# Four edits and a new set of offsets in a planned attention-plus-two-FFN kernel on one core

## The chip, the cores and the metric

The kernel runs on one core of one Trainium2 chip. The metric is device microseconds of one execution; the figure quoted is the median of three runs. The profile comes from one further execution, of which both the device time and the span (first to last instruction) are given.

## The reference, cut to what matters

A delta-rule attention (4 batches, 8 heads, 768 tokens, head width 48) gives 3072 rows of 384, and two feed-forward layers (384 to 2048 to 384) follow.

```python
for t in range(S):                       # 768 steps, state (B, H, 48, 48)
    y[:, :, t] = q_t @ state
    state = state + bt * outer(kt, vt - state.T @ kt)    # kt of norm 1
x = y as (3072, 384)
h = x @ w1_in;  x = np.maximum(0.01 * h, h) @ w1_out
h = x @ w2_in;  out = (h - np.tanh(h)) @ w2_out
```

## The kernel before, in words

The sequence is cut into 12 chunks n of 64 tokens, and two neighbouring chunks form a pair u = n // 2. For each pair the kernel normalises the keys (`keys`, for pair 0 `first_keys`), turns them so that the head width lies on the partitions (`t_batch`), and multiplies them with themselves (`g_batch`, the grams). It inverts a unit triangular matrix for each of the heads (`inverses`: 32x32 blocks, column by column on VectorE), and `merges` joins two blocks into the matrix T: a first round of 32x32 matmuls into PM, a second one whose result is copied into the corner of T. Each chunk then goes through `queries`, `products`, `states` (the recurrence from chunk to chunk) and `outputs`, which leaves x, 256 tokens (two per partition) by 384.

The FFN works on these 256 tokens at a time, once per layer, so there are 24 layer runs. All its matmuls are fp16 with every operand as a pair hi + lo and three products (hi hi, hi lo, lo hi). `to_xa` prepares x of the first layer: a sum of squares on ScalarE, a matmul with ones that spreads the total over the partitions (`norm_sum`), a power-of-two scale (`pow2_scale`), the hi part on ScalarE and the lo part on VectorE, and then a turn by DMA (for chunk 0 by TensorE). `to_xb` does so between the layers. A layer run has 8 steps: `h_part` (18 matmuls of 256 columns, L609 in the profile, into ps_h) and, three steps later, `o_part` (12 of 384 columns into ps_o).

The weights arrive as 64-bit words and are converted at the start by `weight`: three VectorE operations a part (`w_f32`), a sum of squares, a scale and the split into hi and lo. Matrices 0 and 1 (first layer) come first, 2 and 3 after.

Nothing is issued in the order of the code. Every instruction is recorded as a node (L609 and L612 are the two lines that issue all of them), and a planner (`tails`, `schedule`) orders each engine's queue from its cost tables, from the room in the rings of buffers and from the table `BIAS`, an offset for each stage and chunk. So an engine's queue is a fixed list, in which work of several stages is interleaved. Ring `s_r` (six rooms, "sx" in the profile) serves the FFN's intermediate results, the hi and lo parts and the landing tiles of turned keys; ring `ps_a` has four PSUM banks for all small matmuls.

Two ranges matter for the keys. For chunks in `K_DMA` (2 to 11) `t_batch` makes an fp16 pair of the keys (four VectorE and ScalarE operations into KH), turns both halves by DMA into landing tiles of `s_r`, and adds them on VectorE into the fp32 tile kt. For the others (0 and 1) it multiplies with an identity in fp32 and copies two PSUM banks into kt. `M8` (pairs 2 to 5) are the pairs whose merges use eight tiles of the array at a time; pairs 0 and 1 use four.

```python
hi, lo = (KH[:, c_, :, :, 0:D] for c_ in range(2))        # L1010, chunks in K_DMA
    copy(hi[:, :, g], kn[:, :, g])                        # ScalarE
    tt(lo[:, :, g], kn[:, :, g], hi[:, :, g], ALU.subtract)
    turn(land[c_]..., KH[:, c_]...)                       # DMA transpose on SP's queue
tt(kt..., land[0], land[1], ALU.add)
```

Of the kernel before, what the change touches and what calls it, by code (L numbers as in the profile page):

```python
# [19 lines left out]
KS = 64.0  # L20
# [10 lines left out]
def layers(n):  # L31
# [11 lines left out]
OUTB = range(2, 12)  # L43
TRACE = ()
# [3 lines left out]
K_DMA = range(2, 12)  # L48
# [8 lines left out]
    ('consts', 0): -2.8, ('dma', 'b', 0): -10.37, ('dma', 'b', 1): 39.25, ('dma', 'grams', 10): 0.6,  # L57
    ('dma', 'grams', 11): -45.81, ('dma', 'grams', 2): 61.53, ('dma', 'grams', 3): -110.94,
    ('dma', 'grams', 4): 13.52, ('dma', 'grams', 5): -1.77, ('dma', 'grams', 6): 46.0,
    ('dma', 'grams', 7): -43.11, ('dma', 'grams', 8): -183.14, ('dma', 'grams', 9): -82.57,  # L60
    ('dma', 'k', 0): 8.15, ('dma', 'k', 1): 85.3, ('dma', 'keys', 10): -62.96, ('dma', 'keys', 11): 11.27,
    ('dma', 'keys', 2): 130.34, ('dma', 'keys', 3): -19.83, ('dma', 'keys', 4): -117.06,
    ('dma', 'keys', 5): -51.02, ('dma', 'keys', 6): -0.27, ('dma', 'keys', 7): -41.62,
    ('dma', 'keys', 8): -33.98, ('dma', 'keys', 9): -40.04, ('dma', 'o_part1', 0): -113.06,
# [7 lines left out]
    ('dma', 'queries', 0): -146.73, ('dma', 'queries', 1): 17.69, ('dma', 'queries', 10): -116.19,
    ('dma', 'queries', 11): 10.95, ('dma', 'queries', 2): -28.97, ('dma', 'queries', 3): -147.71,
    ('dma', 'queries', 4): -53.56, ('dma', 'queries', 5): 11.09, ('dma', 'queries', 6): -62.06,
    ('dma', 'queries', 7): 5.92, ('dma', 'queries', 8): -44.59, ('dma', 'queries', 9): 63.43,
    ('dma', 'to_xa', 1, 1): -72.81, ('dma', 'to_xa', 10, 1): -8.26, ('dma', 'to_xa', 11, 1): 154.84,
    ('dma', 'to_xa', 2, 1): 2.93, ('dma', 'to_xa', 3, 1): 5.4, ('dma', 'to_xa', 4, 1): 32.04,
    ('dma', 'to_xa', 5, 1): 3.58, ('dma', 'to_xa', 6, 1): 16.44, ('dma', 'to_xa', 7, 1): -144.99,
    ('dma', 'to_xa', 8, 1): -22.03, ('dma', 'to_xa', 9, 1): 22.28, ('dma', 'to_xb', 0, 1): -131.12,
    ('dma', 'to_xb', 1, 1): -169.83, ('dma', 'to_xb', 10, 1): -107.58, ('dma', 'to_xb', 11, 1): 50.71,  # L80
    ('dma', 'to_xb', 2, 1): -7.15, ('dma', 'to_xb', 3, 1): -6.01, ('dma', 'to_xb', 4, 1): -20.2,
    ('dma', 'to_xb', 5, 1): 65.65, ('dma', 'to_xb', 6, 1): -16.83, ('dma', 'to_xb', 7, 1): -97.29,
    ('dma', 'to_xb', 8, 1): 34.46, ('dma', 'to_xb', 9, 1): -4.63, ('dma', 'v', 0): -65.53,
    ('dma', 'weight', 0, 0): -46.39, ('dma', 'weight', 0, 1): -40.51, ('dma', 'weight', 0, 2): -23.2,
    ('dma', 'weight', 0, 3): 21.56, ('dma', 'weight', 0, 4): 56.7, ('dma', 'weight', 0, 5): -5.62,
    ('dma', 'weight', 1, 0): -159.92, ('dma', 'weight', 1, 1): -183.08, ('dma', 'weight', 1, 2): -28.75,
    ('dma', 'weight', 1, 3): -35.61, ('dma', 'weight', 1, 4): -172.45, ('dma', 'weight', 1, 5): -164.56,
    ('dma', 'weight', 2, 0): -32.76, ('dma', 'weight', 2, 1): -6.37, ('dma', 'weight', 2, 2): 4.29,
    ('dma', 'weight', 2, 3): -15.49, ('dma', 'weight', 2, 4): -23.36, ('dma', 'weight', 2, 5): -0.69,
    ('dma', 'weight', 3, 0): 5.74, ('dma', 'weight', 3, 1): -258.17, ('dma', 'weight', 3, 2): -95.47,  # L90
    ('dma', 'weight', 3, 3): -26.22, ('dma', 'weight', 3, 4): 24.43, ('dma', 'weight', 3, 5): -55.49,
    ('first_keys', 0): 59.37, ('grams', 0): 63.14, ('grams', 0, 1): 177.07, ('grams', 1): -205.35,
# [10 lines left out]
    ('h_part1', 9): -0.9, ('inverses', 0): 47.06, ('inverses', 0, 1): 30.6, ('inverses', 1): -11.12,  # L103
    ('inverses', 1, 1): -390.76, ('inverses', 2): -4.07, ('inverses', 2, 1): 225.04, ('inverses', 3): 19.08,
    ('inverses', 3, 1): -0.34, ('inverses', 4): 42.84, ('inverses', 4, 1): -93.8, ('inverses', 5): 2.69,
    ('inverses', 5, 1): -33.82, ('k', 0): -3.88, ('k', 1): -69.27, ('keys', 10): 147.22, ('keys', 11): 55.65,
    ('keys', 2): -18.98, ('keys', 3): -163.15, ('keys', 4): 65.04, ('keys', 5): -252.2, ('keys', 6): 84.49,
    ('keys', 7): -27.36, ('keys', 8): 67.06, ('keys', 9): -58.78, ('merges', 0): -11.68, ('merges', 1): 195.64,
    ('merges', 2): 144.45, ('merges', 3): 2.47, ('merges', 4): -7.63, ('merges', 5): -10.32,
# [16 lines left out]
    ('states', 6, 2): -20.49, ('states', 7): 1.72, ('states', 7, 1): -230.9, ('states', 7, 2): 48.97,
# [1385 lines left out]
```

## Time and profile before

| | |
|---|---|
| median of 3 runs (lowest, highest) | 966.23 us (964.88, 966.59) |
| profiled execution, device time | 965.78 us |
| its span | 963.6 us |
| busy share of TensorE, VectorE, ScalarE | 93%, 63%, 52% |
| mean granted TensorE clock | 0.969 of full speed |

Shares of the whole span hide that this kernel has two parts. In the first 110 us the weights and the first pairs are prepared; from then on the FFN's matmuls run. The rows below are read part by part.

### The profile page before, as it was taken

The page shows a single profiled execution, that of the slowest core. Times are in us where ns is not written, and L with a number is a line of the kernel's source. Part 1 is how long each engine was busy: PE and PEld are TensorE (multiplying, and loading weights), DVE is VectorE, ACT ScalarE, POOL GpSimd, SP SyncE. Part 2 cuts the span into 40 slices and gives each one's busy share as a digit, 9 for nine tenths or more (in the row PEclk, how much of TensorE's full clock was granted, in tenths as well). Part 3 has the DMA queues.
Part 4 walks back from the last instruction along what each step waited for, and adds up shares of the span by engine and source line. Part 5 has one row for each costly group of instructions (what it writes and reads, how often), then busy time and mean ns, then how long its engine had stood idle before and what let it go on. Part 6 is the DMA issues. An engine that isn't in the chain of part 4 may idle for free.

```text
span 963.6 us, 29002 instructions
## 1 busy us (share of the span) xinstructions
PE 896.5 (93%) x12756; PEld 677.5 (70%) x12756; DVE 608.6 (63%) x1332; ACT 499.5 (52%) x1187; POOL 4.9 (1%) x22
## 2 busy tenths in 40 slices
PE   2346899999999999999999999999999999999997
PEld 2215777778777777777777777777777768777675
DVE  7999999987984458953253598499322344512342
ACT  7657767666357566346362427544334434524342
POOL 1000000000000000000000000000000000000000
PEclk9586799999999999999999999999999999999999
DMA  9983673325022432121012111212021000300000
GB/s 349 402 235 104 193 181 116 108 67 95 23 74 59 71 90 64 21 56 36 18 41 33 55 41 36 50 31 56 17 56 18 3 19 17 52 1 18 17 18 16
DMA packets 86718, 71.30 MB, mean 74 GB/s; under 512 B 61760, under 2 KB 73024, under 8 KB 86592
## 3 DMA queue, kind: packets, MB, share of 16 engines
q1 hardware_dynamic: 86592, 69.46, 27.1%
q8 instruction: 99, 1.62, 0.7%
q14 instruction: 27, 0.22, 0.1%
HBM read 44.14 MB, written 4.72 MB: 51 GB/s over the span
## 4 chain that ended last, share of the span: by engine, by line
PE 79%; DVE 13%; ACT 4%; issue 2%; DMA 1%; SPq 1%; ACTq 0%; DVEq 0%
PE ps_h L609 36%; PE ps_o L609 35%; PE ps_a L609 8%; DVE xi L612 3%; DVE wo L612 3%; DVE wi L612 3%; DVE gd L612 2%; ACT gd L612 1%; DVE g L612 1%; DMA wo<-in_w_in_dram 1%; ACT sx L612 1%; DVE sx L612 1%; ACT XW L612 1%; ACT jk L612 1%; ACT wo L612 1%
## 5 line engine op out<-in xcount | busy, mean ns | idle before, releaser
L609 PE MATMUL ps_h<-x,wi 128*128 128x256 f16 x3456 | 403.6, 273 | 3.1 <-ACT sx L612 2.6
L609 PE MATMUL ps_o<-wo,g 128*128 128x384 f16 x2304 | 400.9, 326 | 0.2 <-issue 0.2
L609 PEld LDWEIGHTS <-wi 128*128 128x128 f16 x3456 | 334.9, 98 | 57.3 <-issue 4.5
L609 PEld LDWEIGHTS <-g 128*128 128x128 f16 x2304 | 221.9, 98 | 132.9 <-issue 0.5
L612 ACT ACTIVATE g<-sx 128x512 f16<-128x512 f32 x192 | 120.3, 628 | 113.0 <-PE ps_o L609 57.6
L612 DVE TENSOR_TENSOR g<-sx,g 128x512 f16<-128x512 f32 x96 | 66.0, 688 | 112.6 <-ACT g L612 112.0
L612 DVE SCALAR_TENSOR_TENSOR sx<-sx,kap,ps_h 128x512 f32<-128x512 f32 x96 | 71.2, 744 | 66.8 <-ACT sx L612 66.3
L612 ACT ACTIVATE sx<-ps_h 128x512 f32<-128x512 f32 x96 | 56.7, 592 | 91.8 <-PE ps_h L609 63.2
L612 ACT ACTIVATE sx<-ps_h,kap 128x512 f32<-128x512 f32 x96 | 65.1, 681 | 73.7 <-PE ps_h L609 63.4
L612 DVE SCALAR_TENSOR_TENSOR g<-sx,g 128x512 f16<-128x512 f32 x96 | 66.0, 688 | 36.4 <-ACT g L612 36.0
L612 DVE TENSOR_TENSOR gd<-xi 128x30 f32<-128x30 f32 (+9 forms) x180 | 59.2, 329 | 3.5
L612 DVE TENSOR_TENSOR xi<-xi,gd 128x30 f32<-128x30 f32 (+9 forms) x180 | 59.1, 329 | 3.5
L612 ACT ACTIVATE jk<-kf 128x48 bf16<-128x48 f32 x160 | 38.4, 240 | 14.3 <-DMA kf<-in_k_dram 10.7
L612 ACT ACTIVATE sx<-x,sxs 128x768 f16<-128x768 f32 (+1 forms) x26 | 22.7, 881 | 22.1 <-DVE sxs L612 22.1
L612 ACT ACTIVATION_READ_ACCUMULATOR jk<-kf 128x1 f32 x160 | 30.0, 187 | 0.0
L612 DVE SCALAR_TENSOR_TENSOR wi<-wo,wi 128x768 int32<-128x768 int32 x32 | 29.8, 950 | 0.0
L609 PE MATMUL ps_a<-q,kt 48*64 48x64 f32 x768 | 15.1, 229 | 13.8 <-DMA q<-in_q_dram 11.4
L612 DVE SCALAR_TENSOR_TENSOR sx<-x,sxs,sx 128x768 f16<-128x768 f32 (+1 forms) x26 | 24.6, 951 | 4.6 <-ACT sx L612 4.4
L612 ACT ACTIVATE sx<-x 128x768 bf16<-128x768 f32 x24 | 20.2, 840 | 13.7 <-DVE x L612 13.4
L612 ACT ACTIVATE gd<-ps_a 32x256 f32<-32x256 f32 (+1 forms) x72 | 23.9, 373 | 5.2 <-PE ps_a L609 4.6
L609 PEld LDWEIGHTS ps_a<-q,kt 48*64 48x64 f32 x768 | 13.3, 142 | 16.6 <-ACT wo L612 11.5
L612 DVE TENSOR_SCALAR sx<-ps_o,kap 128x384 f32<-128x384 f32 x12 | 7.4, 618 | 27.5 <-PE ps_o L609 25.5
(124 smaller groups left out, 730.2 us busy)
## 6 DMA issues: line engine op xcount, KB each, us to landing
wo<-in_w_in_dram SPq DMA_DIRECT2D x32, 384.0 KB, 7.8
q<-in_q_dram SPq DMA_DIRECT2D x12, 512.0 KB, 4.5
wi<-in_w_out_dram SPq DMA_DIRECT2D x14, 384.0 KB, 7.8
kf<-in_k_dram SPq DMA_DIRECT2D x12, 384.0 KB, 3.4
vf<-in_v_dram SPq DMA_DIRECT2D x12, 384.0 KB, 3.4
out_dram<-sx SPq DMA_DIRECT2D x48, 96.0 KB, 2.2
x<-in_w_out_dram SPq DMA_DIRECT2D x10, 384.0 KB, 4.0
b<-in_beta_dram SPq DMA_DIRECT2D x6, 512.0 KB, 4.7
```

Source lines behind the costliest of these rows:

```text
L609: self.eng["pe"].matmul(out=o.real(), lhsT=lhsT.real(), rhs=rhs.real(), start=start, stop=stop)
L612: getattr(self.eng[n.on], op)(**{k: v.real() if isinstance(v, View) else v for k, v in kw.items()})
```

## The change

`K_DMA` becomes range(4, 12): chunks 2 and 3 (the second pair) get their keys turned by TensorE, as chunks 0 and 1 did. `PAIRS` is new: for chunks 4 to 11 `g_batch` multiplies the two landing tiles of fp16 keys in three products instead of the fp32 tile kt with itself (kt is still made, for `products` and `states`). `merges` of pairs 0 and 1 does its two rounds and their copies for one half of the heads and then for the other, each under a stage of its own; pairs 2 to 5 are as before. `to_xa` takes a scale for each token instead of one for the 256: two sums of squares, one for each token of a partition, no `norm_sum`, and the hi and lo parts in two operations each for every chunk (before, for chunks 0 and 1 only). `to_xb` multiplies by the inverse of that scale as it copies the layer's result, and `kappa` has one operation less. The table `BIAS` is new in all its values, and some constants of the planner's cost tables change. `SPLIT` and `BY_PE`, with the code that they guard, are empty.

```diff
+SPLIT = ()
+BY_PE = ()
+PAIRS = range(4, 12)
-K_DMA = range(2, 12)
+K_DMA = range(4, 12)
 BIAS = {
-    ('consts', 0): -2.8, ('dma', 'b', 0): -10.37, ('dma', 'b', 1): 39.25, ('dma', 'grams', 10): 0.6,
+    ('consts', 0): -163.33, ('dma', 'b', 0): -14.31, ('dma', 'b', 1): 4.88, ('dma', 'grams', 10): 101.49,
...
     def pow2_scale(o, sq, top, inv=None, by=1):
-        t = g_.tile(p2_r, [128, 2], F32)
-        ts(t[:, 0:1], sq, 2.0 ** -80, None, ALU.max)
+        w = o.shape[1]
+        t = g_.tile(p2_r, [128, 4], F32)
+        ts(t[:, 0:w], sq, 2.0 ** -80, None, ALU.max)
...
             tt(kt.rearrange("p m h i -> p (m h i)"), land[0], land[1], ALU.add)
+            land_t[n] = [t.rearrange("p (m h i) -> p m h i", m=GM, h=2) for t in land]
             return
...
         for m in range(GM):
+            if n in PAIRS:
+                for a, b in ((0, 0), (0, 1), (1, 0)):
+                    for g, h in TILES:
+                        node = mm(ps2[g][HS[h], m], land[a][HD[g], m, h], land[b][HD[g], m, h], a + b == 0, a == 1)
+                continue
             for g, h in TILES:
-                mm(ps2[g][HS[h], m], kt[HD[g], m, h], kt[HD[g], m, h])
+                node = mm(ps2[g][HS[h], m], kt[HD[g], m, h], kt[HD[g], m, h])
...
+        else:
+            for f in range(2):
+                g_.stage = "merges", u, f
+                for jobs, out in ((first, middle), (second, corner)):
+                    ps = bank(HB)
+                    g_.cut()
+                    for m in range(GM):
+                        for h in range(2):
+                            jobs(ps, m, m + f * GM, HQ[2 * h], HQ[2 * h + 1], *spots(f, h))
+                    out(f, ps)
...
-        if n in BOTH or i:
+        if i:
             copy(w[0], x, scale)
             lo_of(w[1], x, scale, w[0])
         else:
-            for k in range(2):
-                ks = slice(k * KT * 128, (k + 1) * KT * 128)
-                copy(w[0][:, ks], x[:, ks], scale)
-                lo_of(w[1][:, ks], x[:, ks], scale, w[0][:, ks])
+            for k in range(HB2):
+                hi, lo, xk = (rows_of(t)[:, k] for t in (*w, x))
+                copy(hi, xk, scale[:, k:k + 1])
+                lo_of(lo, xk, scale[:, k:k + 1], hi)
...
-        pow2_scale(sx[:, 0:1], squares(x), XT)
-        xa_t[n] = x_turn(n, 0, x, sx[:, 0:1]), sx
+        sx = g_.tile(sx_r, [128, 6], F32)
+        acc = norm_acc()
+        junk = g_.tile(s_r, [128, KT * N], BF16)
+        for k in range(HB2):
+            square_sum(acc[:, k:k + 1], rows_of(x)[:, k], rows_of(junk)[:, k])
+        pow2_scale(sx[:, 0:2], acc, XT, sx[:, 2:4])
+        xa_t[n] = x_turn(n, 0, x, sx[:, 0:2]), sx
...
-            cp(rows_of(x)[:, k], po[k][:, 0:DM].rearrange("p (t f) -> p t f", t=KT))
+            cp(rows_of(x)[:, k], po[k][:, 0:DM].rearrange("p (t f) -> p t f", t=KT), sx[:, 2 + k:3 + k])
...
-        tt(kap[:, 1:2], sx[:, 0:1], sw[:, 0:1], ALU.mult)
-        ts(kap[:, 1:2], kap[:, 1:2], sw[:, 1:2], C0, ALU.mult, ALU.mult)
+        ts(kap[:, 1:2], sw[:, 0:1], sw[:, 1:2], C0, ALU.mult, ALU.mult)
```

## Rows read from the trace of the kernel before

**Rows 1.** The page, parts 1 and 2: busy time; VectorE in 40 slices.
```profile
PE 896.5 (93%) x12756; PEld 677.5 (70%) x12756; DVE 608.6 (63%) x1332; ACT 499.5 (52%) x1187; POOL 4.9 (1%) x22
...
DVE  7999999987984458953253598499322344512342
```

**Rows 2.** Windows: us, busy of PE, PEld, DVE, ACT, POOL, clock, DMA share, GB/s.
```profile
24.00:110.00 86.00, 46.51 (x1053) 33.70 (x1053) 84.84 (x181) 54.62 (x135) 0.22 (x2) 0.67 0.71 237
...
110.00:205.00 95.00, 92.48 (x903) 69.88 (x904) 92.14 (x203) 69.96 (x172) 0.00 (x0) 1.00 0.48 134
205.00:955.00 750.00, 747.96 (x10526) 566.45 (x10525) 413.31 (x908) 356.43 (x810) 0.00 (x0) 1.00 0.18 39
```

**Rows 3.** TensorE's timeline at the start: start us, us, what, idle before it.
```profile
13.02 3.50 PE L609 MATMUL ps_a<-ident,kf 64*64 64x64 f32 x128 [13.02 <-DVE kf L612]
...
74.84 0.28 PE L609 MATMUL ps_a<-gd,AT 32*32 32x32 f32 x2 [9.29 <-DVE gd L612]
...
111.34 4.10 PE L609 MATMUL ps_h<-x,wi 128*128 128x256 f16 x36
```

**Rows 4.** VectorE's timeline, 59 to 62 us.
```profile
59.52 0.55 DVE L612 TENSOR_TENSOR KH<-kf,KH 128x384 f16<-128x384 f32 x1
59.99 0.35 DVE L612 TENSOR_TENSOR xi<-xi,gd 128x198 f32<-128x198 f32 x1
60.26 1.22 DVE L612 TENSOR_TENSOR kt<-sx,sx 128x1024 f32<-128x1024 f16 x1
61.40 0.55 DVE L612 TENSOR_TENSOR KH<-kf,KH 128x384 f16<-128x384 f32 x1
```

**Rows 5.** Tiles KH and kt: duration ns min/median/max, first and last start us.
```profile
L612 ACT ACTIVATE KH<-kf x20: 506/521/535, 46.7 to 609.9; 128x384 f16<-128x384 f32 x20
L612 DVE TENSOR_TENSOR KH<-kf,KH x20: 536/551/559, 47.5 to 610.4; 128x384 f16<-128x384 f32 x20
L612 SPq DMA_TRANSPOSE sx<-KH x20: 1231/1264/2247, 54.4 to 612.8; - x20
...
L612 ACT ACTIVATE kt<-ps_a x4: 579/592/604, 15.6 to 17.5; 128x512 f32<-128x512 f32 x4
```

**Rows 6.** TensorE's timeline in the FFN's part, two short stretches.
```profile
501.53 0.17 PE L609 MATMUL ps_a<-ab,ones 128*128 128x1 bf16 x1
501.56 8.94 PE L609 MATMUL ps_o<-wo,g 128*128 128x384 f16 x54
...
542.96 1.16 PE L609 MATMUL ps_a<-kt 48*64 48x64 f32 x64
543.94 1.10 PE L609 MATMUL ps_a<-vf,XW 64*64 64x48 f32 x64
```

**Rows 7.** The chain that ended last: start us, us, what.
```profile
541.06 1.97 PE ps_h L609 x18
```

**Rows 8.** Window of one merge round, matmuls into ps_a alone.
```profile
597.60:598.90 1.30, 1.27 (x128) 1.00 0.78 151
```

**Rows 9.** Groups of instructions, shapes apart: busy us, mean ns, idle before.
```profile
L612 ACT ACTIVATE sx<-x,sxs 128x768 f16<-128x768 f32 x22 | 20.5, 931 | 20.6 <-DVE sxs L612 20.6
L612 ACT ACTIVATE sx<-x 128x768 bf16<-128x768 f32 x24 | 20.2, 840 | 13.7 <-DVE x L612 13.4
...
L612 DVE SCALAR_TENSOR_TENSOR sx<-x,sxs,sx 128x768 f16<-128x768 f32 x22 | 22.3, 1012 | 4.6 <-ACT sx L612 4.4
...
L612 ACT ACTIVATION_READ_ACCUMULATOR sx<-x 128x1 f32 x24 | 4.5, 187 | 0.0
...
L612 ACT ACTIVATE x<-ps_o 128x384 f32<-128x384 f32 x17 | 8.1, 488 | 11.6 <-PE ps_o L609 11.6
...
L612 ACT ACTIVATE sx<-ps_o,kap 128x384 f32<-128x384 f32 x12 | 7.0, 582 | 24.5 <-PE ps_o L609 24.5
...
L612 DVE SCALAR_TENSOR_TENSOR sx<-x,sxs,sx 128x384 f16<-128x384 f32 x4 | 2.4, 618 | 0.0
L612 ACT ACTIVATE sx<-x,sxs 128x384 f16<-128x384 f32 x4 | 2.2, 607 | 1.6 <-DVE sxs L612 1.6
```

More of the change, by code (lines that the diff above doesn't have):

```diff
@@ L72 @@
[L72 to L92, printed above, removed]
@@ L104 @@
[L104 to L108, printed above, removed]
@@ new lines @@
+    ('dma', 'to_xb', 6, 1): 30.41, ('dma', 'to_xb', 7, 1): 111.33, ('dma', 'to_xb', 8, 1): -5.54,
+    ('dma', 'to_xb', 9, 1): 25.08, ('dma', 'v', 0): 188.11, ('dma', 'weight', 0, 0): 102.19,
+    ('dma', 'weight', 0, 1): 3.36, ('dma', 'weight', 0, 2): 132.54, ('dma', 'weight', 0, 3): 117.63,
+    ('dma', 'weight', 0, 4): -16.2, ('dma', 'weight', 0, 5): 80.41, ('dma', 'weight', 1, 0): 91.92,
+    ('dma', 'weight', 1, 1): -0.96, ('dma', 'weight', 1, 2): -8.96, ('dma', 'weight', 1, 3): 30.51,
+    ('dma', 'weight', 1, 4): 68.57, ('dma', 'weight', 1, 5): -61.18, ('dma', 'weight', 2, 0): 28.71,
@@ new lines @@
+    ('dma', 'weight', 2, 1): 271.97, ('dma', 'weight', 2, 2): -57.8, ('dma', 'weight', 2, 3): 84.26,
+    ('dma', 'weight', 2, 4): 4.81, ('dma', 'weight', 2, 5): -63.5, ('dma', 'weight', 3, 0): 187.16,
+    ('dma', 'weight', 3, 1): 43.21, ('dma', 'weight', 3, 2): -1.14, ('dma', 'weight', 3, 3): -34.18,
+    ('dma', 'weight', 3, 4): 5.8, ('dma', 'weight', 3, 5): 12.7, ('first_keys', 0): -47.37,
+    ('grams', 0): -14.98, ('grams', 0, 1): 48.35, ('grams', 1): 1.53, ('grams', 1, 1): -39.36,
+    ('grams', 10): 59.18, ('grams', 10, 1): 14.84, ('grams', 11): -57.53, ('grams', 11, 1): -8.67,
@@ new lines @@
+    ('grams', 2): -1.14, ('grams', 2, 1): -5.92, ('grams', 3): 26.94, ('grams', 3, 1): 3.32,
+    ('grams', 4): 86.46, ('grams', 4, 1): 0.9, ('grams', 5): 0.44, ('grams', 5, 1): 5.39, ('grams', 6): 25.72,
+    ('grams', 6, 1): 76.52, ('grams', 7): -0.97, ('grams', 7, 1): 3.03, ('grams', 8): 200.86,
+    ('grams', 8, 1): -7.11, ('grams', 9): 16.53, ('grams', 9, 1): 86.75, ('h_part0', 1): 92.74,
[5 rows of a table added]
+    ('inverses', 0, 1): 60.51, ('inverses', 1): -122.39, ('inverses', 1, 1): -29.23, ('inverses', 2): -5.65,
@@ new lines @@
+    ('inverses', 2, 1): -114.59, ('inverses', 3): -8.4, ('inverses', 3, 1): -23.04, ('inverses', 4): -65.3,
+    ('inverses', 4, 1): -29.24, ('inverses', 5): -207.32, ('inverses', 5, 1): -65.75, ('k', 0): -10.23,
+    ('k', 1): -92.56, ('keys', 10): 19.56, ('keys', 11): 4.63, ('keys', 2): 470.28, ('keys', 3): 144.52,
+    ('keys', 4): 141.17, ('keys', 5): 69.28, ('keys', 6): -57.57, ('keys', 7): 60.03, ('keys', 8): 88.12,
+    ('keys', 9): -10.08, ('merges', 0, 0): 18.95, ('merges', 0, 1): -15.3, ('merges', 1, 0): 22.87,
@@ new lines @@
+    ('states', 9, 2): -47.2, ('to_xa', 0): 488.96, ('to_xa', 0, 1): 199.02, ('to_xa', 1): 165.29,
+    ('to_xa', 10): -69.28, ('to_xa', 11): -4.7, ('to_xa', 2): -125.51, ('to_xa', 3): -0.79,
+    ('to_xa', 4): -26.42, ('to_xa', 5): -6.82, ('to_xa', 6): 131.42, ('to_xa', 7): 34.95, ('to_xa', 9): 0.76,
+    ('to_xb', 0): -21.99, ('to_xb', 1): 31.08, ('to_xb', 10): 107.44, ('to_xb', 11): -24.99,
+    ('to_xb', 2): 71.92, ('to_xb', 3): 65.9, ('to_xb', 4): 61.95, ('to_xb', 5): 12.27, ('to_xb', 6): 3.78,
@@ new lines @@
+    ('to_xb', 7): 67.17, ('to_xb', 8): 13.14, ('to_xb', 9): 186.55, ('weight', 0): 75.84,
+    ('weight', 0, 0): 41.1, ('weight', 0, 1): -9.85, ('weight', 0, 2): -181.96, ('weight', 0, 3): -45.95,
+    ('weight', 0, 4): -32.36, ('weight', 0, 5): -285.81, ('weight', 1): 55.85, ('weight', 1, 0): -259.48,
+    ('weight', 1, 1): -29.62, ('weight', 1, 2): 67.89, ('weight', 1, 3): -55.02, ('weight', 1, 4): 95.03,
+    ('weight', 1, 5): -126.84, ('weight', 2): 44.53, ('weight', 2, 0): 117.02, ('weight', 2, 1): -335.04,
@@ L141 @@
+    ('weight', 2, 2): 251.85, ('weight', 2, 3): 98.55, ('weight', 2, 4): 119.34, ('weight', 2, 5): -66.58,
+    ('weight', 3): 55.56, ('weight', 3, 0): 208.14, ('weight', 3, 1): -86.56, ('weight', 3, 2): -5.5,
+    ('weight', 3, 3): -75.19, ('weight', 3, 4): -139.71, ('weight', 3, 5): -76.27,
 }
@@ L356, in matmul @@
         node.cnt += 1 + (lhsT.ap.dtype == F32)
-        node.cols += o.free * lhsT.shape[0] / 128
+        node.cols += o.free * lhsT.shape[0] / 128 * (4 if lhsT.ap.dtype == F32 and lhsT.shape[0] > 64 else 1)
         if lhsT.ap.dtype == F32:
@@ L366, in matmul @@
             if lhsT.ap.dtype == F32 and kind in (True, False):
-                kind = 3 if kind else 5
+                kind = 5 if not kind else 6 if lhsT.free > 48 else 7
             node.warm += self.SMALL[kind][0]
@@ L671 @@
     gd_r = ring("gd", 2, MM * HB)
-    xi_r = ring("xi", 1, HB * HB)
+    xi_r = ring("xi", 1, HB * HB + (HB if SPLIT else 0))
     jk_r = ring("jk", 1, D // 2, short=True)
@@ L677 @@
     ab_r = ring("ab", 6, 2, short=True)
-    p2_r = ring("p2", 2, 2, short=True)
+    p2_r = ring("p2", 2, 4, short=True)
     n2_r = ring("n2", 1, 3 * MM)
@@ L766 @@
     maskb = fixed("maskb", [128, 2], F32)
+    half = fixed("half", [128, 4], F32)
     ones = fixed("ones", [128, 2], BF16)
@@ L794, in consts @@
             select(ident2[r], [[1, C]], ALU.is_equal, -1)
+        if SPLIT:
+            dve("tensor_reduce", out=half[:, 2:4], in_=ident2.rearrange("p (b c) -> p b c", b=2)[:, :, HB // 2:], axis=AX.X, op=ALU.add)
+            tt(half[:, 1:2], half[:, 2:3], half[:, 3:4], ALU.add)
+            ts(half[:, 0:1], half[:, 1:2], -1.0, 1.0, ALU.mult, ALU.add)
+        for h in range(2):
+            r = slice(C * h, C * (h + 1))
             select(maskp[r], [[1, C]], ALU.is_gt, -1)
@@ L1029, in g_batch @@
     def g_batch(n, Gd, bt):
-        s, kt = n % 2, kt_t[n]
+        s, kt, land = n % 2, kt_t[n], land_t.pop(n, None)
         ps2 = banks(C)
         for m in range(GM):
-            for g, h in TILES:
-                mm(ps2[g][HS[h], m], kt[HD[g], m, h], kt[HD[g], m, h])
+            if n in PAIRS:
[3 more added lines that the diff above has]
+                continue
+            for g, h in TILES:
+                node = mm(ps2[g][HS[h], m], kt[HD[g], m, h], kt[HD[g], m, h])
+        if s == 0:
+            for t in (Gd, raw_t.get(n // 2)):
+                if t is not None:
+                    g_.claim(node, t)
         for g in range(NG):
@@ L1068, in inverses @@
         bs = b_t.pop((u, 0))
-        X = g_.tile(xi_r, [128, HB, HB], F32)
-        transpose(X.rearrange("p i j -> p j i"), Gd.rearrange("p m j -> p j m"))
-        eng = inv_eng(u)
-        def solve(j, lo, hi):
-            col = X[:, lo:hi, j:j + 1].to_broadcast([128, hi - lo, j])
-            tt(Gd[:, lo:hi, :j], col, X[:, j:j + 1, :j].to_broadcast([128, hi - lo, j]), ALU.mult, (eng,))
-            tt(X[:, lo:hi, :j], X[:, lo:hi, :j], Gd[:, lo:hi, :j], ALU.add, (eng,))
-        for j in range(1, HB - 1):
-            solve(j, j + 1, HB)
+        Xf = g_.tile(xi_r, [128, HB * HB + (HB if SPLIT else 0)], F32)
@@ new lines, in inverses, with turned @@
+        X = Xf[:, 0:HB * HB].rearrange("p (i j) -> p i j", i=HB)
+        def turned(o, src):
+            g_.quad = 3
+            n = HB // 2
+            for c in range(2):
+                ps = g_.tile(ps_a, [128, 512], F32).rearrange("p (j i) -> p j i", j=n)
+                g_.cut()
+                for j in range(n):
+                    for q_ in range(4):
+                        mm(ps[HQ[q_], j], src(c * n + j)[HQ[q_]], ident2[HQ[q_], HB * (q_ % 2):HB * (q_ % 2) + HB])
+                cp(o[:, :, c * n:(c + 1) * n], ps.rearrange("p j i -> p i j"))
+            g_.quad = True
@@ new lines, in inverses, with solve @@
+        eng = inv_eng(u)
+        if u in BY_PE:
+            turned(X, lambda j: Gd[:, :, j])
+        else:
+            transpose(X.rearrange("p i j -> p j i"), Gd.rearrange("p m j -> p j m"))
+        if u in SPLIT:
+            n = HB // 2
+            X4 = Xf.rearrange("p (b w) -> p b w", b=2)[:, :, 0:n * HB].rearrange("p b (i j) -> p b i j", j=HB)[:, :, :, 0:n]
+            G1 = Gd.rearrange("p m j -> p (m j)")
+            for j in range(1, n - 1):
+                w = n - j - 1
+                shape = [128, 2, w, j]
+                t = G1[:, 0:2 * w * j].rearrange("p (b i j) -> p b i j", b=2, i=w)
+                tt(t, X4[:, :, j + 1:, j:j + 1].to_broadcast(shape), X4[:, :, j:j + 1, :j].to_broadcast(shape), ALU.mult)
+                tt(X4[:, :, j + 1:, :j], X4[:, :, j + 1:, :j], t, ALU.add)
+        else:
+            def solve(j, lo, hi):
+                col = X[:, lo:hi, j:j + 1].to_broadcast([128, hi - lo, j])
+                tt(Gd[:, lo:hi, :j], col, X[:, j:j + 1, :j].to_broadcast([128, hi - lo, j]), ALU.mult, (eng,))
+                tt(X[:, lo:hi, :j], X[:, lo:hi, :j], Gd[:, lo:hi, :j], ALU.add, (eng,))
+            for j in range(1, HB - 1):
+                solve(j, j + 1, HB)
@@ L1082, in inverses @@
         ts(X.rearrange("p i j -> p (i j)")[:, 0:HB * HB:HB + 1], bs, 1.0, None, ALU.mult, eng=eng)
-        nat = Gd
-        transpose(nat.rearrange("p m j -> p j m"), X.rearrange("p i j -> p j i"))
-        transpose(XW[:, :, HB:].rearrange("p m i -> p i m"), X)
+        nat, tt_ = Gd, XW[:, :, HB:]
+        if u in BY_PE:
+            turned(nat, lambda j: X[:, :, j])
+            turned(tt_, lambda i: X[:, i])
+        else:
+            transpose(nat.rearrange("p m j -> p j m"), X.rearrange("p i j -> p j i"))
+            transpose(tt_.rearrange("p m i -> p i m"), X)
+        if u in SPLIT:
+            g_.stage = "inverses", u, 2
+            raw, n = raw_t.pop(u), HB // 2
+            g_.quad = 3
+            for f in range(2):
+                ps = g_.tile(ps_a, [128, 512], F32).rearrange("p (m j) -> p m j", m=16)
+                g_.cut()
+                for m in range(16):
+                    for q_ in range(4):
+                        mm(ps[HQ[q_], m], raw[HQ[q_], f * 16 + m], nat[HQ[q_], f * 16 + m])
+                cp(raw[:, f * 16:f * 16 + 16], ps)
+            for o, cols, l, r, mask in ((nat, slice(0, n), tt_, raw, half[:, 1:2]), (tt_, slice(n, HB), raw, tt_, half[:, 0:1])):
+                ps = g_.tile(ps_a, [128, 512], F32).rearrange("p (m j) -> p m j", m=MM)
+                g_.cut()
+                for m in range(MM):
+                    for q_ in range(4):
+                        mm(ps[HQ[q_], m], l[HQ[q_], m], r[HQ[q_], m, cols])
+                stt(o[:, :, cols], ps, mask, o[:, :, cols], ALU.mult, ALU.add)
+            g_.quad = True
         for h in range(2):
@@ L1118, in second, with middle @@
             mm(ps[out_dn, m], nat[up, 2 * i + 1], PM[up, i])
-        ps = rounds(first)
-        for f in range(2):
+        xm = tt_.rearrange("p (m a) i -> p a m i", a=2)
+        def middle(f, ps):
             fm = slice(f * GM, (f + 1) * GM)
@@ L1124, in merges, with corner @@
                 for h in range(2):
-                    cp(PM[HS[h], fm], ps[f][HS[1 - h]])
+                    cp(PM[HS[h], fm], ps[HS[1 - h]])
             else:
-                cp(PM[:, fm], ps[f])
-        ps = rounds(second)
-        g_.quad = True
-        xm = tt_.rearrange("p (m a) i -> p a m i", a=2)
-        for f in range(2):
+                cp(PM[:, fm], ps)
+        def corner(f, ps):
             for a in range(2):
                 for h in range(2):
-                    cp(xm[HQ[2 * h], a][:, f * GM:(f + 1) * GM], ps[f][spots(f, h)[a]], -1.0)
+                    cp(xm[HQ[2 * h], a][:, f * GM:(f + 1) * GM], ps[spots(f, h)[a]], -1.0)
+        if eight:
+            for jobs, out in ((first, middle), (second, corner)):
+                ps = rounds(jobs)
+                for f in range(2):
+                    out(f, ps[f])
+        else:
+            for f in range(2):
+                g_.stage = "merges", u, f
+                for jobs, out in ((first, middle), (second, corner)):
+                    ps = bank(HB)
+                    g_.cut()
+                    for m in range(GM):
+                        for h in range(2):
+                            jobs(ps, m, m + f * GM, HQ[2 * h], HQ[2 * h + 1], *spots(f, h))
+                    out(f, ps)
+        g_.quad = True
     q_t, p_t, u_t = {}, {}, {}
@@ L1318, in to_xb @@
         for k in range(HB2):
-            cp(rows_of(x)[:, k], po[k][:, 0:DM].rearrange("p (t f) -> p t f", t=KT))
-        pow2_scale(sx[:, 1:2], squares(x), XT)
-        xb_t[n] = x_turn(n, 1, x, sx[:, 1:2]), sx
+            cp(rows_of(x)[:, k], po[k][:, 0:DM].rearrange("p (t f) -> p t f", t=KT), sx[:, 2 + k:3 + k])
+        pow2_scale(sx[:, 4:5], squares(x), XT)
+        xb_t[n] = x_turn(n, 1, x, sx[:, 4:5]), sx
     def h_part(n, i, x, p, kap):
@@ L1479, in lay_out @@
     low = (np.arange(128) % 32)[:, None, None] > np.arange(32)
+    near = low & ((np.arange(128) % 32)[:, None, None] // 16 == np.arange(32) // 16)
+    low = np.stack([near if u in SPLIT else low for u in range(U)])
     bt = np.concatenate([
```

107 lines of the change are left out of this document (50 added, 57 removed), and 26 rows, old and new, of the table BIAS.

## The prediction

> **What bounds the kernel now.** The page comes first. TensorE is busy 93% of the span, and VectorE's slices are full at the start only [rows 1]: two parts with different limits, so no share of the whole span prices this change. I cut the span into windows next, and set the cuts by TensorE's timeline. The first FFN matmul starts at 111.34 us [rows 3]. From 24 to 110 us VectorE is busy 84.84 of 86.00 us and TensorE 46.51; from 110 to 205 us both are full (92.14 and 92.48 of 95.00); from 205 to 955 us TensorE is busy 747.96 of 750.00 us and VectorE and ScalarE about half the time [rows 2].
>
> The reader is to see a queue handed over. Until about 205 us VectorE is the bound: it converts four weight matrices and runs the inverses of the first pairs, and the FFN can start only as early as this work allows. From 111 us on TensorE has no holes to close: 2.0 us idle in 750. So the time is the start of the FFN, plus TensorE's work after it, plus a short tail. An edit pays only if it takes work off VectorE before some 205 us (the FFN then starts earlier), or off TensorE after 111 us. On ScalarE, or on VectorE late, it is free within wide limits.
>
> The sum is made against the profiled execution: device time 965.78 us, span 963.6. The median of the runs shown is 966.23, 0.45 above; I add that at the end. About 0.2%, 1.9 us, is what a measurement of this kernel can tell from no change.
>
> **The second pair's keys by TensorE.** Two chunks leave the DMA path. Removed from VectorE: four subtractions into KH and two additions into kt. The timeline shows them between the column steps of the first inverse, with no hole beside them [rows 4]. Their durations are 0.55 and 1.22 us, but the next instruction starts 0.47 us after the subtraction; with the same 0.08 us of overlap, the addition takes 1.14. So 4 x 0.47 + 2 x 1.14 = 4.16 us of a full engine. Removed elsewhere: four hi copies of 0.52 us on ScalarE, and four transposes that hold SP's queue for 1.26 us each [rows 5], 5.1 us in which a weight piece behind them can't be issued. Added: 128 small TensorE instructions, which cost 3.50 us for chunks 0 and 1 [rows 3], and four copies into kt, 0.59 us each [rows 5]. TensorE's part is hidden: it has a hole of 9.29 us up to 74.84 us [rows 3] and is half idle there [rows 2]; without that cover it would cost 3.5 us. ScalarE gains 4 x (0.59 - 0.52) = 0.3 us on 54.62 of 86 us. Two bounds: the whole 4.16 us comes off the start of the FFN, or nothing does, because another chain (ScalarE, the landing of the weights) ends last. I take 4.2, since VectorE has 1.2 us of idle in 86 and nobody else is near that.
>
> **Grams from fp16 pairs.** For each of 8 chunks, 64 instructions (32 fp32 matmuls in two passes each) become 96. The 64 take 543.94 - 542.96 = 0.98 us, 15.3 ns each [rows 6]. No row shows a small fp16 matmul. From below: 256 fp16 columns at full array take 1.97 / 18 = 109.4 ns [rows 7], so 64 columns take 27.4, and four tiles at a time make 6.8 ns: 0.66 us for the 96, which saves 0.32 us a chunk, 2.6 us in all. From above: the same 15.3 ns as an fp32 instruction, 1.47 us, a loss of 0.49 us a chunk, 3.9 us in all. The nearest row of a shorter instruction is the 32x32 one, 1.27 us for 128, 9.9 ns [rows 8]. I take that: 0.95 us, so no change. The landing tiles are held until these matmuls are done instead of until the addition, two of the six rooms of `s_r` for a few us; ScalarE and VectorE have half their time free there [rows 2], so I price that at nothing; if a step of the FFN missed its room it would cost at most the step's 18 matmuls, 1.97 us, each time.
>
> **The scale by token.** For each chunk `norm_sum` goes: the matmul with ones starts at 501.53 us and the next at 501.56 [rows 6], 0.03 us of TensorE, 0.3 us over the 11 chunks that fall in the full part. ScalarE gains a second sum of squares: two halves of about 0.55 us (an estimate: 840 ns shortened as 931 is to 607) with a read of 0.19 each, against 0.84 + 0.19: 0.45 us. For chunks 2 to 11 the split gains 2 x 0.607 - 0.931 = 0.28 us on ScalarE and 2 x 0.618 - 1.012 = 0.22 on VectorE; the copies of `to_xb` gain 0.09 each, by the row of a copy with a scale against one without [rows 9]. `pow2_scale` has one small operation more, `kappa` one less. All of it lies on engines with 40% idle, under a full TensorE, and costs nothing; without cover it would be under 1 us a chunk. On the way to the first x the saved trip through TensorE and the longer sums of squares cancel.
>
> **The corners by chunk.** Pairs 0 and 1 have the same matmuls and copies, in another order: the first half's copies can run while TensorE does the second half. In a stage where VectorE sets the pace I price this at nothing; it could give up to the 1.27 us of one round [rows 8] if the chain of the first pair set the start, and can't lose more, since the order inside a half is unchanged.
>
> **The offsets.** A new table changes the order on every queue. It can't add or remove work. After 205 us it can close at most the 2.0 us of holes; before, it may hand copies that either engine can do to ScalarE, which has 31 us free of 86 [rows 2], or place the first x better. Bounds: 6 us earlier (about as much again as the keys give), or 4 us later (two FFN steps of 1.97 us without their input). I take zero.
>
> The sum: 965.8 - 4.2 - 0.3 + 0 = 961.3; with 0.45 for the median, 961.7 us.
>
> **The rivals.** *More comes of the start.* If the new order also shortens the way to the first x, or moves copies from VectorE, the offsets' 6 us and the 1.3 of the corners add: down to 954 us. For it: ScalarE's free third, and the 39 us in which TensorE idles between 24 and 110 us [rows 2]. Against: VectorE's weight work can't move, and must end by the time the second layer begins.
>
> *The change doesn't do what it says.* The FFN doesn't start earlier although VectorE has less to do, because the start waits for the landing of weights or ScalarE's conversions; then only the 0.3 us remain: 965.9 us. For it: the DMA share is 0.71 up to 110 us [rows 2]. Against: TensorE and ScalarE there mostly wait for VectorE.
>
> *Slower, by the price of a small instruction.* The change adds 8 x 32 = 256 instructions to the full TensorE. If the price goes by count, at 15.3 ns or more, and not by columns, the grams cost 3.9 us and eat the start's gain: 965.6 us. It turns slower than 968.2 us when 768 fp16 instructions cost 8 x 0.98 + 6.5 = 14.3 us, from 18.7 ns each on. If the four tiles did not run side by side at all, 27.4 ns each, the grams would cost 21.0 us instead of 7.8, and the time would be 974.9 us. Against: 32x32 instructions go at 9.9 ns [rows 8], which no fixed 15 ns allows. I give this mechanism 0.07. The Trainium skill (TensorE: Matmul & The Clock Gate, section "Wait — 56ns, not 53.3ns?") speaks for it: it says that starts of matmuls never come closer than about 25 ns, however few the columns. By that page's figure the 96 would take 2.4 us, an estimate, and the sum would be 11.4 us more, 973 us. The trace does not agree: its starts are 15.3 and 9.9 ns apart, so the floor does not hold where tiles take turns.
>
> **How the numbers follow.** The forecast (959 to 964 us) 0.42; more from the start (953 to 959) 0.24; no earlier start, or the gain eaten within the measurement, 0.17; slower 0.17: the instructions' price 0.07, an order that leaves the FFN unfed 0.10. So faster 0.66, same 0.17, slower 0.17. The range, 953 to 968.5, leaves out the far ends of the first rival and the larger part of the slower case; the likeliest alone has 959 to 964.
>
> **What would show it.** Right: KH has 16 operations per engine instead of 20, and 16 transposes; the first matmul into ps_h starts near 107 us; VectorE stays full up to about 200 us; TensorE's idle between 205 and 955 us stays near 2 us; a gram of chunks 4 to 11 has 96 instructions and takes 0.7 to 1.1 us. Wrong: the first ps_h matmul at 111 us or later (the start waits for another engine), a gram over 1.8 us (the instruction's price), or TensorE idle after 205 us that grows by several us with ScalarE's "sx" as releaser (rooms of `s_r`, or the order).

## The result and the profile after

The changed kernel takes 956.24 us (median of 4 executions, 954.46 to 956.92), the kernel before 966.41 beside it: a ratio of 0.9895, interval 0.9878 to 0.9912, 10.2 us faster. Medians and ratios in this document leave out executions in a slow state, with a lower clock: one of e3's, and e4's profiled one. The profiled execution took 956.11 us, with a span of 954.4. The page's parts 1 and 2, which answer to [rows 1], with the granted clock:

```profile
span 954.4 us, 29725 instructions
...
PE 896.9 (94%) x13128; PEld 677.0 (71%) x13128; DVE 597.6 (63%) x1330; ACT 505.7 (53%) x1227; POOL 5.0 (1%) x24
...
DVE  7999999995697445983343697453793244232342
...
PEclk9577899999999999999999999999999999999999
```

In this execution TensorE is busy as long as before, 896.9 us to 896.5, with 372 instructions more, and the gain is time in which it stood idle. That split is of this execution alone: in a second one of the same kernel (e11) TensorE is busy for 892.4 us (see the last section). The windows of [rows 2]:

```profile
24.00:110.00 86.00, 49.74 (x1052) 35.52 (x1052) 84.06 (x178) 64.03 (x191) 0.22 (x2) 0.70 0.66 234
110.00:205.00 95.00, 94.97 (x1022) 71.31 (x1020) 92.25 (x217) 69.12 (x177) 0.00 (x0) 1.00 0.50 129
205.00:955.00 750.00, 743.49 (x10740) 561.94 (x10737) 404.31 (x897) 362.13 (x839) 0.00 (x0) 1.00 0.19 39
```

TensorE's timeline, answering to [rows 3]: the second pair's keys in a hole (two groups, 64 of its 128 instructions), and the first FFN matmul at 98.78 us instead of 111.34, where 107 was forecast.

```profile
79.17 0.68 PE L613 MATMUL ps_a<-ident,kf 64*64 64x64 f32 x28 [0.15 <-ACT u L616]
80.36 0.80 PE L613 MATMUL ps_a<-ident,kf 64*64 64x64 f32 x36 [0.50 <-issue]
...
98.78 5.05 PE L613 MATMUL ps_h<-x,wi 128*128 128x256 f16 x27
```

That start is 12.6 us earlier and the span only 9.2 shorter, so the start is no measure of the gain. A better one is how much of the FFN is done when VectorE's full part ends, at 205 us. Windows of the matmuls into ps_h and then of those into ps_o, before:

```profile
98.00:205.00 107.00, 49.45 (x414) 0.95 0.49 139
...
98.00:205.00 107.00, 46.10 (x262) 0.95 0.49 139
```

And after:

```profile
98.00:205.00 107.00, 54.95 (x453) 0.98 0.49 131
...
98.00:205.00 107.00, 47.19 (x276) 0.98 0.49 131
```

39 matmuls of ps_h at 0.109 us [rows 7] and 14 of ps_o at 0.166 [rows 6] are 6.6 us of work that is no longer due behind 205 us. There the cheaper grams save 1.4 us (below), and TensorE is not busy for 749.4 - 743.5 = 5.9 us up to the end, against 758.6 - 751.4 = 7.2 before. 6.6 + 1.4 + 1.3 = 9.3, beside the 9.2 of the spans; with the 0.3 of the matmuls with ones, which the change removes, it is 9.6, so the account closes to half a us.

A gram of 96 fp16 instructions in after's timeline, its first and its last rows and what follows (answers to [rows 6]):

```profile
372.90 0.21 PE L613 MATMUL ps_a<-sx 48*64 48x64 f16 x4
372.93 0.24 PE L613 MATMUL ps_a<-sx,sx 48*64 48x64 f16 x8
...
373.55 0.22 PE L613 MATMUL ps_a<-sx 48*64 48x64 f16 x4
373.58 0.25 PE L613 MATMUL ps_a<-sx,sx 48*64 48x64 f16 x8
373.65 0.22 PE L613 MATMUL ps_a<-sx 48*64 48x64 f16 x4
...
373.87 0.83 PE L613 MATMUL ps_h<-x,wi 128*128 128x256 f16 x6
```

From 373.55 to 373.65 twelve start in 0.10 us, 8.2 ns each; the forecast took 9.9.

### The profile page after: what moved, and what is told of

It is laid out like the page before. It is cut to its first block, busy times and chain, and to the rows that moved or that the text cites. A ratio compares the mean times of both kernels' runs of the same rounds, so it can differ in the third digit from the quotient of the medians.

```text
span 954.4 us, 29725 instructions
## 1 busy us (share of the span) xinstructions
PE 896.9 (94%) x13128; PEld 677.0 (71%) x13128; DVE 597.6 (63%) x1330; ACT 505.7 (53%) x1227; POOL 5.0 (1%) x24
## 4 chain that ended last, share of the span: by engine, by line
PE 86%; DVE 9%; DMA 2%; issue 1%; ACT 1%; SPq 0%; DVEq 0%; ACTq 0%
PE ps_o L613 39%; PE ps_h L613 38%; PE ps_a L613 9%; DVE gd L616 2%; DVE xi L616 2%; DMA wo<-in_w_in_dram 2%; DVE wi L616 2%; DVE wo L616 1%; DVE sx L616 1%; DVE p L616 0%; DVE g L616 0%; DVE XW L616 0%; ACT XW L616 0%; SPq L616 0%; DVE S L616 0%
## 5 line engine op out<-in xcount | busy, mean ns | idle before, releaser
L613 PE MATMUL ps_o<-wo,g 128*128 128x384 f16 x2304 | 396.6, 326 | 0.2 <-DVE sx L616 0.2
L616 ACT ACTIVATE sx<-x,sxs 128x384 f16<-128x384 f32 (+1 forms) x36 | 25.2, 715 | 21.2 <-DVE sxs L616 21.0
L616 DVE SCALAR_TENSOR_TENSOR sx<-x,sxs,sx 128x384 f16<-128x384 f32 (+1 forms) x36 | 26.7, 749 | 5.1 <-ACT sx L616 4.6
L616 ACT ACTIVATE sx<-x 128x384 bf16<-128x384 f32 (+1 forms) x36 | 22.4, 623 | 13.5 <-DVE g L616 7.2
L616 ACT ACTIVATE XW<-ps_a 32x256 f32<-32x256 f32 x46 | 17.2, 375 | 13.8 <-PE ps_a L613 13.3
L613 PE MATMUL ps_a<-wi,unit_s 128*128 128x384 f32 x32 | 16.8, 612 | 6.1 <-ACT unit_s L616 4.7
```

The lines of the kernel that those rows point to most:

```text
L613: self.eng["pe"].matmul(out=o.real(), lhsT=lhsT.real(), rhs=rhs.real(), start=start, stop=stop)
L616: getattr(self.eng[n.on], op)(**{k: v.real() if isinstance(v, View) else v for k, v in kw.items()})
```

## The experiments

Two theories. T1, the order: the offsets make the gain, by putting work that the first x doesn't need behind it. T2, the code: the edits make it. A planner that is given one edit less plans everything anew, so in all experiments the plan is replaced by a written list of nodes and buffer rooms:

```diff
-    order, _ = g_.schedule(g_.tails())
+    by = dict(p="pe", a="act", d="dve", g="pool", s="sp")
+    order = []
+    for w in FIXED.split():                  # "1203p 988d ...": node, engine
+        n = g_.nodes[int(w[:-1])]
+        n.on = by[w[-1]]
+        order.append(n)
+        for b in n.new:
+            b.slot = int(ROOMS[b.ring.name][b.rank])
```

The list is that of after's or of before's plan; a node that the other kernel lacks stands where its inputs are ready. Ratios are to the kernel before on the same chip; 0.001 is 0.97 us. After has 0.9895, and 0.9884 (0.9868 to 0.9901) in a second measurement (e11, 955.32 us), 0.98895 in the mean; each difference below has an uncertainty of 1.5 to 2 us.

**Whole code, whole order, crossed.** e1 is before's code in after's order, e2 after's code in before's order.

> The code of before (keys of pair 2 turned by DMA, one scale for a chunk, joint corners, fp32 grams) issued in the order of after's plan; a step that after lacks stands where its inputs are ready. Theory T1, the order: the 12.6 us of the start come for two thirds or more from work that the new order puts behind the first x; then the first ps_h matmul starts at 100 to 104 us (98.8 plus the 4.2 us of the keys and little else), against 111.3 for before, and the time is 958 to 963 us if the borrowed order leaves no holes later. Theory T2, the code: the four edits make the start early and the order alone doesn't; the first ps_h matmul stays at 107 to 111 us and the time at 964 us or more. The start decides, since holes behind 205 us can come from an order made for other steps.

> The code of after issued in the order of before's plan. T1: the first ps_h matmul starts at 106 to 110 us, since only the 4.2 us of the keys can come off the 111.3; the time is 961 to 966 us, more if holes appear behind 205 us. T2: the first ps_h matmul starts at 98 to 102 us as in after, and the time is 956 to 959 us.

Measured: e1 974.38 us (1.0087, interval 1.0072 to 1.0102), first ps_h matmul at 103.4 us; e2 973.77 (1.0076, 1.0063 to 1.009), at 110.5. The start of e1 fits T1, that of e2 misses T1's 106 to 110 by half a us, and the times fit neither theory: both are slower than before.

**One edit taken back, in after's order.** e3: `K_DMA = range(2, 12)`. e4 and e4b: `PAIRS = ()`. e5: `to_xa`, `to_xb` and `kappa` with one scale, as before. e6: in `merges`, `if eight:` becomes `if True:`.

> After, with the keys of the second pair turned by DMA again (four subtractions, two additions back on VectorE), everything else in after's order. T1: the first ps_h matmul at 100 to 103 us, the time 2 to 4 us above after (958 to 960 us). T2, keys as the main cause: the first ps_h matmul at 104 us or later and the time 6 us or more above after (962 us or more).

> After, with all grams of the later chunks as fp32 matmuls of summed tiles again, everything else in after's order. After's timeline has a gram of 96 fp16 instructions in about 0.79 us, before's one of 64 fp32 instructions in 0.98 us. If the price is so, 8 grams give 1.5 us and this kernel takes 957.0 to 958.5 us. If the grams are worth nothing (the forecast took 9.9 ns an instruction, 0.95 us a gram), it is within 0.5 us of after's 956.2. If VectorE's or ScalarE's part of the edit matters, TensorE's idle time behind 205 us differs by over 1 us from after's.

> The kernel of e4_grams_fp32 once more, for a profile that can be read and a second interval. That run took 960.6 us, 4.4 above after, where 1.5 were expected from the grams' own instructions. If 4.4 is right, either TensorE's instructions behind the first ps_h are 4 us more (the grams price more than 0.98 - 0.79 us each), or TensorE's idle time behind 205 us is 2 to 3 us more than after's 1.5. If it was a stray, this run is at 957.0 to 958.5 us.

> After, with one power-of-two scale for a chunk again in the first layer (sum of squares over all tokens, a matmul with ones, one kappa), everything else in after's order. The forecast priced this at 0.3 us of TensorE and nothing at the start; then the first ps_h matmul stays at 98 to 99.5 us and the time is within 1 us of after. The rival, that the trip through TensorE lies on the way to the first x: the first ps_h matmul 1 to 2 us later and the time 1 to 2 us above.

> After, with the corners of T of pairs 0 and 1 built for both chunks in one round again, everything else in after's order. The forecast priced it at nothing, with a bound of 1.27 us: then the first ps_h matmul stays within 1.3 us of 98.78. The rival, that the first chunk's chain sets the start and the round by chunk lets it go ahead: the first ps_h matmul 2 us or more later.

| taken back | median us | ratio (interval) | over after |
|---|---|---|---|
| keys (e3) | 959.84 | 0.9934 (0.9917 to 0.9952) | 4.3 us |
| grams (e4; e4b) | 960.47; 958.8 | 0.9937 (0.9923 to 0.9951); 0.9928 (0.9914 to 0.9941) | 4.2 us |
| scale (e5) | 957.61 | 0.9913 (0.9898 to 0.9927) | 2.3 us |
| corners (e6) | 967.12 | 1.0011 (1.0002 to 1.0021) | 11.7 us |

The first ps_h matmul starts at 101.0 us in e3, 98.4 in e4b, 97.8 in e5 and 99.7 in e6. e3 came as T1 had it. e4, e4b and e5 cost more than was expected of them.

e6 is too much for an edit with the same work. TensorE's timeline has its holes between 217 and 249 us, the longest here:

```profile
229.25 1.15 PE L773 MATMUL ps_a<-vf,XW 64*64 64x48 f32 x64
...
248.91 0.22 PE L773 MATMUL ps_a<-sx 48*64 48x64 f16 x4 [3.48 <-ACT XW L776]
```

After does the same vf,XW matmuls at 218.54 us. ScalarE's timeline of e6 says why: of the first half's four copies into XW the last stands 8 us behind the others, after copies of the FFN's steps (two of four shown).

```profile
218.49 1.17 ACT L776 ACTIVATE XW<-ps_a 32x256 f32<-32x256 f32 x3 [1.31 <-PE ps_a L773]
...
222.06 0.63 ACT L776 ACTIVATE g<-sx 128x512 f16<-128x512 f32 x1 [0.82 <-DVE sx L776]
...
225.97 0.63 ACT L776 ACTIVATE g<-sx 128x512 f16<-128x512 f32 x1 [0.81 <-DVE sx L776]
226.63 0.38 ACT L776 ACTIVATE XW<-ps_a 32x256 f32<-32x256 f32 x1
```

My placing was at fault: with one round for both halves the copies come in another sequence, and the fourth copy of the first half had taken the place of the second half's. e1 has that copy 8 us late too. e8 and e10 put the four copies together, and move up the matmuls that need them:

> e6_corners_joint once more, with one thing changed in the order: there, one of ScalarE's four copies into pair 1's XW stood 8 us behind the other three, behind three steps of the FFN, and the first matmul of the chunk waited for it. Here the four stand together. If the corners by chunk are worth the 10.9 us that e6 showed, the time stays at 964 us or more. If that was the place of one copy, the holes between 217 and 249 us shrink from 7 us to 1 to 3, and the time is 957 to 959.5 us.

> e1_before_code_after_order once more: the code of before in after's order, with ScalarE's four copies into pair 1's XW together, as in e8_corners_joint_mended. The single edits, taken back in after's order, cost 3.7 us (keys), 2.6 to 4.2 (grams), 1.4 (scale) and 1.3 (corners, mended), 9.0 to 10.6 in all. T2, the code: if these are the whole gain, this kernel takes 956.2 + 9 to 10.6 = 965 to 967 us, as before does in its own order, and the order by itself gives nothing. T1, the order: the old code keeps most of the gain, 957 to 961 us.

> The changed kernel itself, beside e10 on one chip, so that the differences of the single edits stand on more than four times of it. Both theories: 955.5 to 957 us, the first ps_h matmul at 98.8 us. If it is 958 us or more, the worth of each edit taken back is smaller by as much.

Measured: e8 957.58 us (0.9898, 0.9882 to 0.9913), so the corners are worth 0.8 us, not told from nothing; one copy of 0.38 us in a wrong place, with the matmuls behind it, had cost 10.9 us (11.7 - 0.8). e10 967.07 us (1.0005, 0.9996 to 1.0015), 11.2 us over after. The four single differences add up to 4.3 + 4.2 + 2.3 + 0.8 = 11.6. T1 falls for this order: the old code gains nothing from it. But the order is not fitted to the old code: from 205 to 800 us TensorE is idle for 4.2 us in e10, for 2.0 before and for 0.8 in after. Yet e10's first ps_h matmul starts at 103.3 us, 8 earlier than before's. Its windows of ps_h and ps_o show what the start hides:

```profile
98.00:205.00 107.00, 53.39 (x432) 0.95 0.51 144
...
98.00:205.00 107.00, 43.94 (x258) 0.95 0.51 144
```

By 205 us it has done 18 matmuls of ps_h more than before and 4 of ps_o less, 1.3 us of work: what the order put behind the start came back there.

**Orders made by the planner's costs.** e7 and e9 take the lists of e10 and of after and move single instructions until the planner's own costs show fewer holes of TensorE.

> The code of before, with an order of its own that starts out from after's: ScalarE's copies of pair 1's corners put where their data are ready, then single instructions moved (and a few copies given to the other engine) so that TensorE's holes by the planner's costs close. None of the four edits is in it. T1, the order: the early start can be had without the edits; the first ps_h matmul starts at 99 to 103 us and the time is 956 to 961 us. T2, the code: without the edits the work that was put behind the start comes back as holes of TensorE; the time is 963 us or more, wherever the first ps_h matmul starts.

> The code of after, with its order worked over in the same way as in e7_before_code_fitted_order. If the order is where time is still to be had, the first ps_h matmul starts at 97.5 to 98.5 us and the time is 953 to 955.5 us, 1 to 3 us under after. If after's order is as good as any, it stays within 1 us of 956.2.

Measured: e7 968.64 us (1.0019, 1.0006 to 1.0033), start 104.5; e9 963.77 (0.9964, 0.995 to 0.9978), start 102.4. e7 comes out as T2 had it; e9 fits neither of its expectations and is some 7 us slower than after. In the window from 24 to 98 us VectorE is busy 68.86 and 70.09 us, in after 72.94: by the planner's costs these lists fit, on the chip VectorE is idle there for 5.1 and 3.9 us instead of 1.1. So it stays open whether a better order exists, for the old code or the new.

**Before's order.** e2 had copies of pair 0's and pair 1's corners out of place too; e12 mends them, e14 is e12 with `PAIRS = ()`, and e13 is the kernel before with `K_DMA = range(4, 12)` alone.

> e2_after_code_before_order once more, with pair 0's and pair 1's corner copies where the old order has those of the same chunk. If the edits carry their gain in any order, and e2 was spoiled by these copies: 956 to 962 us, the first ps_h matmul at 106 to 108 us. If the new code needs an order of its own: 968 us or more, with holes behind 205 us as in e2.

> The kernel before with one edit: the second pair's keys by TensorE, in before's own order, in which nothing else moves. The forecast's step by itself: 4.2 us off VectorE, the first ps_h matmul at 107 us and the time 961.5 to 963 us. The rival, that another chain ends next (e2 began only 0.9 us earlier): the first ps_h matmul at 109.5 us or later and the time 964.5 us or more.

> e12_after_code_before_order_mended with fp32 grams again, so with the keys by TensorE, the scale by token and the corners by chunk, in before's order. If the landing tiles that the fp16 pairs hold are what the old order has no room for: 8 us or more under e12, 958 to 963 us. If not: at e12's time or up to 4 us above it, since the grams' own gain is gone.

Measured: e13 962.87 us (0.9965, 0.9954 to 0.9977), e14 962.28 (0.9958, 0.9944 to 0.9972), e12 970.48 (1.0047, 1.003 to 1.0064). The first ps_h matmul of e13 starts where the forecast had it:

```profile
107.49 4.10 PE L769 MATMUL ps_h<-x,wi 128*128 128x256 f16 x36
```

From e14 to e12 the code of the grams changes, and with it the written list: as the landing tiles are held longer, 239 of the 336 tiles of `s_r` lie in other rooms, and instructions in two stretches of the list stand elsewhere. Together that costs 8.6 us in this order. Where e12's two largest holes are, TensorE waits for ScalarE, and ScalarE for a DMA that still reads the room of `s_r` into which it must write: at 424 us an output DMA (shown), at 363 us, for 2.6 us, the DMA that turns x. e12's profiled execution took 974.67 us, the slowest of its six; e2's has the same wait for the output DMA, 6.7 us in all. TensorE's timeline of e12:

```profile
424.35 1.93 PE L774 MATMUL ps_o<-wo,g 128*128 128x384 f16 x7 [2.51 <-ACT sx L777]
```

ScalarE's timeline:

```profile
423.72 0.58 ACT L777 ACTIVATE sx<-ps_o,kap 128x384 f32<-128x384 f32 x1 [3.32 <-DMA out_dram<-sx]
```

ScalarE's waits between 340 and 430 us (us in total, times, longest), in e12 and then in e14:

```profile
ACT sx L777 <- DMA out_dram<-sx: 6.6, 3, 3.3
```

```profile
ACT sx L777 <- DMA out_dram<-sx: 0.4, 1, 0.4
```

So the longer-held landing tiles fit the old order badly; in after's own profile this wait is 0.9 us in the same stretch. How much of the 8.6 us is due to the rooms as I wrote them, and not to the old order itself, was not separated.

## Why the prediction was right or wrong

**Keys, right.** Forecast: 4.16 us off VectorE come off the FFN's start, which moves to 107 us. e13 shows the step by itself: 107.5 us and 3.4 us of time; taken back in after's order it is 4.3. From 24 us to that start VectorE is busy for 82.30 of 83.40 us in e13, before for 86.14 of 87.30: 3.8 us less work, and as full as it was. In after KH has 16 operations on each engine:

```profile
L616 ACT ACTIVATE KH<-kf x16: 506/514/523, 200.6 to 576.3; 128x384 f16<-128x384 f32 x16
L616 DVE TENSOR_TENSOR KH<-kf,KH x16: 537/553/559, 201.1 to 578.2; 128x384 f16<-128x384 f32 x16
L616 SPq DMA_TRANSPOSE sx<-KH x16: 1231/1237/1571, 202.3 to 583.7; - x16
```

**Grams, the step that failed.** "I take that: 0.95 us, so no change" took 9.9 ns from the nearest row, which is of fp32 and of smaller tiles; an fp16 instruction costs 8.2. From its first start to the next instruction's, a gram lasts 0.79 to 0.97 us in after, 7.12 for the eight, and 0.98 to 1.10 in e4b, 8.52: 1.4 us, inside the bound of 2.6. The measured 4.2, with an uncertainty of 1.5, is more. e4b's timeline has one hole of 1.77 us, inside a group of equal matmuls and with no engine named, that after hasn't:

```profile
600.14 0.56 PE L774 MATMUL ps_a<-S,kt 48*64 48x48 f32 x22
602.46 0.84 PE L774 MATMUL ps_a<-S,kt 48*64 48x48 f32 x42 [1.77 <-issue]
```

e4's profile has it too, 1.54 us before the last 42 of the same 64 matmuls, so it is no chance of one execution; before and e14, with fp32 grams in before's order, have no hole over 0.5 us without an engine named behind 205 us, so it belongs to this list and not to the fp32 instructions alone. With it 3.2 of the 4.2 are found. The cause of the hole stays open; what is shown of the grams' own price is the 1.4 us. The third rival, by which a small instruction keeps its price of 15 ns whatever its columns, is refuted: 8.2 ns for one of 64 columns. The Trainium skill (TensorE: Matmul & The Clock Gate, section "Wait — 56ns, not 53.3ns?") has starts never closer than about 25 ns; this trace, with 8.2 ns, doesn't agree where four tiles take turns.

**Landing tiles.** Priced "at nothing", with 1.97 us for each step that misses its room. In after's order that holds; in before's order, with its rooms written anew, it is 8.6 us, and two of e12's holes are 2.5 us each, above the 1.97. The cover depends on the order and the rooms.

**Scale, too small.** 0.3 us of TensorE was forecast, 2.3 measured (0.5 to 4.1 with its uncertainty), so the excess is barely clear of it. TensorE's idle time from 205 to 800 us is 0.8 us in after, 1.0 in e11 and 2.0 in e5: about 1 us of holes beside the 0.3. That the shorter way to a scale closes them is not shown: e5's largest, 0.79 us, ends on VectorE's sx, the next, 0.54, on no engine.

**Corners, right:** nothing that can be measured, 0.8 us.

**Offsets.** Taken as zero, and by themselves they are: e10 and before differ by 0.5 us, interval -0.4 to 1.4. But they are not an addend. With the new code, before's order takes 970.5 us and after's 956; in before's order the whole change is a loss of 4.5 us. The bounds, 6 us earlier and 4 later, left that out.

**The first rival** had the time, 953 to 959 us, and not its cause: it expected the offsets to shorten the start. The start did come 12.6 us earlier, but e10 has 8 of these and no gain. The sentence behind it, "the time is the start of the FFN, plus TensorE's work after it", let the work behind the start stand still, while an order can move small matmuls across it. It also took TensorE as full from 111 us on; between 110 and 205 us it had 2.5 us of holes (92.48 of 95.00), and after has none (94.97). The sum failed because it gave 0.3 us to three edits worth some 7 together, of which the grams are the larger part.

## What to carry to other kernels

Where a planner orders everything, take one edit back in a list that is held still, and look at each instruction that the list puts elsewhere: one 0.38 us copy behind the wrong step, with what waited for it, was worth some 10 us. Ask of each edit which tile lives longer through it; here that was free in one order and cost 8 us in another. For a hand-over between two stages count the work of the second that is done when the first ends, not when its first instruction starts.

## What was unexpected in the hardware

The FFN's first matmuls can run at half the clock. In after's profiled execution the 27 at 98.78 us took 5.05 us; in e11, the same kernel, the row at 97.23 us has 27 in 3.11:

```profile
97.23 3.11 PE L613 MATMUL ps_h<-x,wi 128*128 128x256 f16 x27
```

The granted clock of the window from 98.78 to 102 us was 0.50 in the first, that from 97.23 to 100 us 1.00 in the second: the levels of 1.2 and 2.4 GHz. TensorE had been idle for half of the time ahead, with a mean clock of 0.68 from 24 to 98 us in after. e11's span is 1.8 us shorter, 952.6, and TensorE's busy time 892.4 instead of 896.9. So one profile of this kernel carries some 2 us of chance in its first part. An early start is the more exposed to it: the first 27 took 4.77 to 5.85 us in the profiles of e3, e5, e8 and e10 too and 3.11 in e4b, while before, e13 and e14, which start at 107 us or later, had a granted clock of 1.00 for their first 36 (4.10 us).
